# Thirty tiny probe loads in the stream of a decode block: one set of 15 amid the loads, one set behind the last

## The chip, the cores and the metric

The kernel runs on one NeuronCore of a Trainium2 chip. The metric is the device time of one execution in microseconds; the number given for a kernel is the median of its runs. A profile of one execution lies beside the times: it lists the instructions of the engines TensorE (PE), VectorE (DVE), ScalarE (ACT), GpSimd (POOL) and SyncE (SP), and the packets of the core's 16 DMA engines.

## The reference

One decode step (one token, batch 2, width 640) of a conditioned transformer block. Six modulation vectors come from a condition c; attention reads the last 1,024 of 4,096 cached positions, with 32 heads of 192; a gated FFN of width 1,536 follows. All inputs are bf16.

```python
def reference(A_x, A_k_cache, A_v_cache, A_wq, A_wo, B_x, B_w_gate, B_w_up, B_w_down, c, w_mod):
    # A: attention
    W = min(4096, max(256, Sk // 4))                     # 1024
    q = (h @ wq) per head
    k, v = k_cache[:, :, Sk - W:, :], v_cache[:, :, Sk - W:, :]
    p = softmax(einsum('bhqd,bhkd->bhqk', q, k) * Dh ** (-0.5))
    A = einsum('bhqk,bhkd->bhqd', p, v) reshaped @ wo
    # the block
    x = A_x
    mod = (silu(c) @ w_mod).reshape(2, 6, 1, -1)         # sa, ca, ga, sb, cb, gb
    h = layernorm(x) * (1 + ca) + sa
    x = x + ga * A(h)
    h = layernorm(x) * (1 + cb) + sb
    x = x + gb * ((gelu(h @ w_gate) * (h @ w_up)) @ w_down)
    return x
```

## The kernel before, in words

The kernel reads 76.9 MB from HBM once and does little with each byte: a K element is multiplied and summed, a V element and a weight are used in one matrix product. Nearly everything that is read goes into one big SBUF tile, `arena`, of seven slots, whose places are reused as soon as their contents are consumed.

There are 17 large loads, all issued by SP through `k_dma` (line 290), each over all 128 partitions. Their order is that of the dictionary `place`: w_mod; wq; the three pieces of K for batch 0, called k(0,0), k(0,1), k(0,2); then v(0,0), k(1,0), v(0,1), k(1,1), v(1,0), v(1,1); then wo, w_gate, w_up, and w_down in three pieces of 8, 3 and 1 row blocks (`WD_SPLIT`). A row of a load (one partition's share) is 1,280 to 61,440 B long. The function `pump` (line 333) writes the queue: it appends the next load to SP's list as long as the arena places that it overlaps have been named as consumed, and the recording class `_Sched` adds the wait on the engine that last used those places. SP runs its list strictly in order, so a load that waits holds up those behind it. Two tiny loads, c (`crow`, two rows) and x (`xr`, eight rows), and the store of the result (`st_out`, line 685) are issued by ACT.

Beside the stream the engines work as the data arrive. PE multiplies the modulation (line 454) and the query projection (line 486). For K, DVE multiplies a chunk by the broadcast query in place (line 512), PE sums it over the head's elements with an identity matrix (line 524), and DVE reduces the rest (line 531). Then comes the softmax of one batch (lines 536 to 555). For V, DVE spreads the probabilities over a mask (line 561) and PE multiplies (line 575). After v(1,1) come wo (line 634), the second layernorm, the gate and up products (line 655), the down product (line 675), two DVE steps (lines 681 and 683) and the store.

Every large load has a semaphore of its own, raised to 16 on completion. The four compute engines count on one semaphore each. At the end (lines 688 to 702) the waits are resolved, the first load is moved ahead of the entry barrier, and the lists are emitted engine by engine; SP gets a last wait for the store.

Of the kernel before, what the change touches and what calls it, by code (L numbers as in the profile page):

```python
# [8 lines left out]
BF16 = mybir.dt.bfloat16  # L9
# [110 lines left out]
def bass_adaLN_cond__sliding_block_cached__geglu_ffn__decode_kernel(  # L120
# [51 lines left out]
    WD_SPLIT = [(0, 8), (8, 3), (11, 1)]  # L172
# [15 lines left out]
    with es:  # L188
        S = _Sched(nc, es)
        sb = lambda name, shape, dt: es.enter_context(nc.sbuf_tensor(name, shape, dt))  # L190
# [10 lines left out]
        for kind, b, t, z in tiles:  # L201
            j0, n = (K_SPLIT if kind == "k" else V_SPLIT)[b][t]
# [86 lines left out]
        def k_dma(dst, src):  # L289
            return lambda e: e.dma_start(dst, src)  # L290

        items = list(place)
        assert items[0] == ("wm", 0)
        queue = {"next": 0, "done": set(), "ops": {}}

        def overlap(x, y):
            (a, m), (b, n) = place[x], place[y]
            return a < b + n and b < a + m

        def keys(it, lo=0, width=None):  # L300
            o, n = place[it]
            width = n - lo if width is None else width
            assert lo + width <= n
            return [("ar", z) for z in range((o + lo) // UNIT, -(-(o + lo + width) // UNIT))]

        def view(it, lo=0, width=None):
            o, n = place[it]
            width = n - lo if width is None else width
            return arena[:, o + lo:o + lo + width]

        def source(it):
            kind = it[0]
            if kind == "wm":
                return w_mod.rearrange("(p k) n -> p (k n)", k=KT)
            if kind == "wq":
                k0, n = WQ_SPLIT[it[1]]
                return A_wq.rearrange("(p k) n -> p (k n)", k=KT)[:, k0 * NQ:(k0 + n) * NQ]
            if kind == "wo":
                t0, n = WO_SPLIT[it[1]]
                return A_wo.rearrange("(p t) n -> p (t n)", t=NT)[:, t0 * D:(t0 + n) * D]  # L320
            if kind == "wg":
                return B_w_gate.rearrange("(p k) n -> p (k n)", k=KT)
            if kind == "wu":
                k0, nk = WU_SPLIT[it[1]]
                return B_w_up.rearrange("(p k) n -> p (k n)", k=KT)[:, k0 * F:(k0 + nk) * F]
            if kind == "wd":
                r0, nr = WD_SPLIT[it[1]]
                return B_w_down.rearrange("(p r) n -> p (r n)", r=FC)[:, r0 * D:(r0 + nr) * D]
            b, (j0, n) = it[1], span[it]
            src = A_k_cache if kind == "k" else A_v_cache  # L330
            return src[b][:, K0:Sk, :].rearrange("h (x j) d -> h x j d", x=XQ)[:, :, j0:j0 + n, :].rearrange("h x j d -> h x (j d)")

        def pump(*consumed):
            queue["done"].update(consumed)
            while queue["next"] < len(items):
                n = queue["next"]
                it = items[n]
                if not all(x in queue["done"] for x in items[:n] if overlap(x, it)):
                    break
                queue["ops"][it] = S.dma("sp", k_dma(view(it), source(it)), sem_of[it], writes=keys(it), name="ld_%s" % "_".join(str(z) for z in it))  # L340
                queue["next"] += 1

        pump()
        wm_dma = queue["ops"][("wm", 0)]
        S.op("pool", lambda e: e.memset(xr[:, :], 0.0), writes=["xr"], name="xr0")
# [102 lines left out]
        for half in range(2):  # L448
# [15 lines left out]
            if half == 0:  # L464
                ln_mod("ln1", 0, 0, hT)
        pump(("wm", 0))

        def out_rows(src, key, dst_t, name):
# [9 lines left out]
        for w, (k0, nk) in enumerate(WQ_SPLIT):  # L478
            def f(e, w=w, k0=k0, nk=nk):
                last = None  # L480
                wv = view(("wq", w)).rearrange("p (k i n) -> p k i n", k=nk, i=NR)
                for kk in range(nk):
                    k = k0 + kk
                    for n in range(NQB):
                        for i in range(NR):
                            last = e.matmul(ps[32 * i:32 * i + B, n, :], lhsT=hT[:, k, 0:RM:RB], rhs=wv[:, kk, i, n * QW:(n + 1) * QW],  # L486
                                            start=(k == 0), stop=(k == KT - 1), tile_position=(0, 32 * i))
                return last
            S.op("pe", f, reads=["ln1_out"] + keys(("wq", w)), writes=[bank(n) for n in range(NQB)], name="q1_%d" % w)
            pump(("wq", w))  # L490
# [205 lines left out]
        del body[n0:]  # L696
        body[entry:entry] = moved
        S.emit("sp", nc.sync, tail=lambda e: e.wait_ge(sem_out, 16))
        S.emit("pool", nc.gpsimd)
        S.emit("act", nc.scalar)  # L700
        S.emit("dve", nc.vector)
        S.emit("pe", nc.tensor)
        held, size = {}, None
# [41 lines left out]
```

## Time and profile before

| What | Value |
|---|---|
| Median of 3 runs | 185.7 us (185.64 to 185.83) |
| Span of the profiled execution, first to last instruction | 184.6 us |
| Difference of the median and this span | 1.1 us |
| Read from HBM | 76.88 MB, 417 GB/s over the span |
| PE busy | 106.4 us (58%) |
| DVE busy | 107.3 us (58%) |
| ACT, POOL busy | 14.4 us (8%), 6.1 us (3%) |
| Mean granted TensorE clock | 0.884 |
| DMA packets in the span | 2,495 |

The profiled execution's own time is its span of 184.6 us and what lies around it, before the first and after the last instruction; the page gives the span. A queue in the profile (q1 is SP's, q10 ACT's, q8 and q14 bring instructions) has a ring on each of the 16 DMA engines. A load shows there as its rows, one packet each, followed on every engine that takes part by a packet of 4 B, the completion write to the load's semaphore. An engine's packets of one queue run in the order of issue; packets of two queues take turns.

### The profile page before, as it was taken

How to read it: one execution, taken by the hardware profiler on the slowest of the kernel's cores; microseconds unless marked ns; L12 is line 12 of the kernel's file. 1: busy time of each engine (PE TensorE's matmuls, PEld its weight loads, DVE VectorE, ACT ScalarE, POOL GpSimd, SP SyncE). 2: the span in 40 equal slices, each digit the busy share in tenths (PEclk: the TensorE clock that was granted, in tenths of full speed). 3: DMA queues.
4: the chain of work that ended last, by engine and by line, in shares of the span. 5: the costliest groups of instructions: out<-in, count | busy, mean ns of one | idle time of the engine just before them, and what ended most of it. 6: DMA issues, size and time to landing. Idle time of an engine off the chain costs nothing.

```text
span 184.6 us, 1862 instructions
## 1 busy us (share of the span) xinstructions
PE 106.4 (58%) x960; PEld 28.9 (16%) x693; DVE 107.3 (58%) x105; ACT 14.4 (8%) x27; POOL 6.1 (3%) x23
## 2 busy tenths in 40 slices
PE   0019000948663096662499665946662499898833
PEld 0012000120000000001260001500001356405213
DVE  6022200049993488965993999489975838300631
ACT  2041100050000000001000000000001000220410
POOL 8400000000000000000000000000000000000000
PEclk9999955699999859999589999999998559999995
DMA  8999998999898989899898989898999999979991
GB/s 292 492 496 426 426 426 357 442 426 488 368 501 352 501 362 501 384 460 469 384 490 366 490 362 490 373 490 373 479 405 447 506 443 426 426 316 403 434 376 40
DMA packets 2495, 76.99 MB, mean 417 GB/s; under 512 B 310, under 2 KB 440, under 8 KB 568
## 3 DMA queue, kind: packets, MB, share of 16 engines
q1 hardware_dynamic: 2448, 76.87, 97.1%
q8 instruction: 6, 0.10, 0.2%
q10 hardware_dynamic: 40, 0.01, 0.0%
q14 instruction: 1, 0.01, 0.0%
HBM read 76.88 MB, written 0.00 MB: 417 GB/s over the span
## 4 chain that ended last, share of the span: by engine, by line
DMA 58%; DVE 24%; PE 16%; ACT 1%; issue 1%; SPq 0%
DMA arena<-in_A_k_cache_dram 36%; DMA arena<-in_B_w_down_dram 14%; DVE arena L512 14%; PE ps L575 8%; DMA arena<-in_w_mod_dram 8%; DVE S_sb L531 6%; PE ps L524 3%; DVE Em L561 2%; PE ps L454 2%; PE ps L675 1%; DVE negm L541 1%; ACT E_sb L549 1%; PE ps L552 1%; PE ps L545 0%; DVE M L537 0%
## 5 line engine op out<-in xcount | busy, mean ns | idle before, releaser
L524 PE MATMUL ps<-arena,ident_b 128*128 128x512 bf16 x192 | 48.9, 395 | 29.2 <-DVE arena L512 29.2
L512 DVE TENSOR_TENSOR arena<-arena,qbc 128x3072 bf16<-128x3072 bf16 x32 | 54.8, 1750 | 10.2 <-DMA arena<-in_A_k_cache_dram 8.5
L575 PE MATMUL ps<-arena,Em 128*64 128x384 bf16 x256 | 26.1, 374 | 5.6 <-DVE Em L561 5.6
L531 DVE TENSOR_REDUCE S_sb<-ps 128x32 f32<-128x1024 f32 x16 | 19.5, 1218 | 7.1 <-PE ps L524 7.1
L575 PEld LDWEIGHTS ps<-arena,Em 128*64 128x64 bf16 x256 | 16.2, 126 | 30.7 <-DVE Em L561 22.0
L561 DVE TENSOR_TENSOR Em<-E_sb,maskE 128x2048 bf16<-128x2048 bf16 x8 | 18.0, 2282 | 3.9 <-PE ps L575 3.9
L486 PE MATMUL ps<-arena,hT 128*2 128x512 bf16 x60 | 5.1, 517 | 14.0 <-DMA arena<-in_A_wq_dram 14.0
L496 DVE CAST qrow<-ps 128x512 bf16<-128x512 f32 x1 | 0.7, 691 | 17.4 <-PE ps L486 17.4
L539 PEld LDWEIGHTS ps<-ident_f,M 128*1 128x1 f32 x2 | 0.2, 79 | 61.1 <-DVE M L537 61.1
L408 PE MATMUL ps<-Em,ident_b 128*128 128x512 bf16 x41 | 9.3, 379 | 0.0
L641 DVE TENSOR_TENSOR lnt<-ps,modR 128x160 f32<-128x160 f32 x1 | 0.3, 323 | 12.7 <-PE ps L634 12.7
L549 ACT ACTIVATE E_sb<-S_sb,nbias 128x256 bf16<-128x256 f32 x2 | 1.0, 507 | 66.7 <-DVE nbias L547 66.7
L454 PE MATMUL ps<-arena,scT 128*17 128x480 bf16 x40 | 4.2, 602 | 2.1 <-DMA arena<-in_w_mod_dram 2.1
L582 ACT ACTIVATE On<-ps,rden 128x384 bf16<-128x384 f32 x2 | 1.2, 580 | 49.2 <-PE ps L575 49.2
L634 PEld LDWEIGHTS ps<-arena,oT 128*17 128x17 bf16 x192 | 3.3, 91 | 7.4 <-DMA arena<-in_A_wo_dram 7.4
L396 PE MATMUL ps<-ident_b,crow 2*128 2x2 bf16 x5 | 0.4, 177 | 6.5 <-DMA crow<-in_c_dram 6.5
L634 PE MATMUL ps<-arena,oT 128*17 128x160 bf16 x192 | 3.5, 233 | 0.6 <-DMA arena<-in_A_wo_dram 0.6
L417 PE MATMUL ps<-st,selstat 128*128 128x2 f32 x4 | 0.9, 298 | 4.9 <-ACT sqj L413 4.9
L401 DVE CAST X<-xr 128x160 f32<-128x160 bf16 x1 | 0.2, 243 | 5.8 <-DMA xr<-in_A_x_dram 5.8
L486 PEld LDWEIGHTS ps<-arena,hT 128*2 128x2 bf16 x20 | 0.6, 110 | 18.4 <-issue 18.4
L462 DVE TENSOR_SCALAR opc<-modR 128x160 f32<-128x160 f32 x2 | 0.5, 244 | 4.7 <-ACT modR L459 4.7
L655 PE MATMUL ps<-arena,h2T 128*9 128x384 bf16 x40 | 2.0, 326 | 1.9 <-DMA arena<-in_B_w_up_dram 1.3
(86 smaller groups left out, 51.1 us busy)
## 6 DMA issues: line engine op xcount, KB each, us to landing
arena<-in_A_v_cache_dram SPq DMA_DIRECT2D x4, 6144.0 KB, 26.3
arena<-in_A_k_cache_dram SPq DMA_DIRECT2D x3, 6144.0 KB, 37.5
arena<-in_A_wq_dram SPq DMA_DIRECT2D x1, 7680.0 KB, 31.5
arena<-in_A_wo_dram SPq DMA_DIRECT2D x1, 7680.0 KB, 29.2
arena<-in_A_k_cache_dram SPq DMA_DIRECT2D x2, 3072.0 KB, 42.2
arena<-in_w_mod_dram SPq DMA_DIRECT2D x1, 4800.0 KB, 14.2
arena<-in_B_w_gate_dram SPq DMA_DIRECT2D x1, 1920.0 KB, 21.2
arena<-in_B_w_up_dram SPq DMA_DIRECT2D x1, 1920.0 KB, 22.8
```

The lines of the kernel that those rows point to most:

```text
L408: last = e.matmul(ps[:, BK_T, :], lhsT=ident_b[:, :], rhs=Em[:, 0, 0:512 // H, :].rearrange("p j h -> p (j h)"), start=True, stop=True)
L454: last = e.matmul(ps[32 * i:32 * i + RM, half, 0:MH].rearrange("p (m n) -> p m n", n=DR), lhsT=scT[:, k, :], rhs=wv[:, 3 * half:3 * half + ...
L486: last = e.matmul(ps[32 * i:32 * i + B, n, :], lhsT=hT[:, k, 0:RM:RB], rhs=wv[:, kk, i, n * QW:(n + 1) * QW], start=(k == 0), stop=(k == K ...
L512: S.op("dve", lambda e: e.tensor_tensor(out=kt, in0=kt, in1=qbc[:, b, :].unsqueeze(1).broadcast_to([P, JC, Dh]), op=ALU.mult), reads=[("qb ...
L524: last = e.matmul(o_ap, lhsT=ident_b[:, :], rhs=kt[:, :, t * GC:(t + 1) * GC], start=(t == 0), stop=(t == NCH - 1))
L531: S.op("dve", lambda e: e.tensor_reduce(out=S_sb[:, b, 2 * JC * pair:2 * JC * (pair + 1)], in_=ps[:, 2 * z:2 * z + 2, :].rearrange("p k (j ...
L541: S.op("dve", lambda e: e.tensor_reduce(out=negm[:, b, :].rearrange("p (h x) -> p h x", x=XQ), in_=ps[0:1, BK_T, 0:P].rearrange("p (h x) - ...
L549: S.op("act", lambda e: e.activation(out=E_sb[:, b, :], in_=S_sb[:, b, :], func=ACTF.Exp, scale=SCALE, bias=nbias[:, b:b + 1], accum_out=d ...
L561: S.op("dve", lambda e, z=z, j=j: e.tensor_tensor(out=Em[:, z, :, :], in0=E_sb[:, b, j:j + JE].unsqueeze(2).broadcast_to([P, JE, H]), in1= ...
L575: last = e.matmul(ps[64 * i:64 * i + 2 * H, BK_O, 0:ON], lhsT=Em[:, z, 2 * jp:2 * jp + 2, :].rearrange("p j h -> p (j h)"), rhs=view(it, l ...
L634: last = e.matmul(ps[32 * i:32 * i + RM, 2, 0:DR], lhsT=oT[:, t, :], rhs=wv[:, t, i, :], start=(t == 0), stop=(t == NT - 1), tile_position ...
L655: last = e.matmul(ps[32 * i:32 * i + GM, bk, 0:FT], lhsT=h2T[:, k, 0:RM:2], rhs=wv[:, k, i * FT:(i + 1) * FT], start=(k == 0), stop=(k == ...
```

## The change

A small tile `prb` of 17 partitions is added, and a function `probe`, which issues one load of k rows of 32 B each (16 elements of the first k rows of w_mod) into a place of its own, with a semaphore of its own. After the issue of v(0,0) and again after the issue of the last piece of w_down, `pump` calls it 15 times on SP, for 17 rows, then 2, 3, and so on up to 15 rows. Nothing reads `prb`. So that the program doesn't end before these loads, POOL waits at its end for the first 15 semaphores, and ACT, behind the store's issue, for the other 15.

```diff
+        prb = sb("prb", [17, 30, 16], BF16)
+        probes = []
+
+        def probe(eng, k):
+            n = len(probes)
+            sem = S.sem("d_prb%d" % n)
+            probes.append(sem)
+            S.dma(eng, k_dma(prb[0:k, n, :], w_mod[0:k, 0:16]), sem, writes=[("prb", n)], name="prb%d" % n)
+
         items = list(place)
...
                 queue["ops"][it] = S.dma("sp", k_dma(view(it), source(it)), sem_of[it], writes=keys(it), name="ld_%s" % "_".join(str(z) for z in it))
                 queue["next"] += 1
+                if it in (("v", 0, 0), ("wd", len(WD_SPLIT) - 1)):
+                    for k in (17,) + tuple(range(2, 16)):
+                        probe("sp", k)
...
         S.emit("sp", nc.sync, tail=lambda e: e.wait_ge(sem_out, 16))
-        S.emit("pool", nc.gpsimd)
-        S.emit("act", nc.scalar)
+        S.emit("pool", nc.gpsimd, tail=lambda e: [e.wait_ge(x, 16) for x in probes[:15]])
+        S.emit("act", nc.scalar, tail=lambda e: [e.wait_ge(x, 16) for x in probes[15:]])
```

SP's list grows from 17 loads to 47. The instructions of the other engines keep their order; POOL and ACT each get 8 waiting instructions at their ends, of which all but one wait for two semaphores.

## The prediction

> **What bounds the kernel now.** I read the page's DMA rows first, then its chain, then SyncE's (SP's) waits and DMA issues, and last the individual packet records behind the page (start, length, size and queue of each DMA packet), because the change consists of packets.
>
> From the page (DMA busy share in tenths by slice; queue, packets, MB, share of 16 engines; the chain):
>
> ```profile
> DMA  8999998999898989899898989898999999979991
> ...
> q1 hardware_dynamic: 2448, 76.87, 97.1%
> q8 instruction: 6, 0.10, 0.2%
> q10 hardware_dynamic: 40, 0.01, 0.0%
> ...
> DMA 58%; DVE 24%; PE 16%; ACT 1%; issue 1%; SPq 0%
> ```
>
> The kernel is one uninterrupted stream on q1, SP's queue: 97.1% of all 16 engines' span, and the missing 3% is the first microsecond and the last five. The chain's 24% DVE and 16% PE are work beside the stream: it follows buffer releases back, and those releases come early. The table by stretch confirms it (stretch, length, then busy time by engine, clock, DMA share, GB/s):
>
> ```profile
> 54.00:84.00 30.00, 17.17 (x60) 0.00 (x0) 21.80 (x16) 0.00 (x0) 0.00 (x0) 0.89 1.01 436
> 84.00:150.00 66.00, 42.09 (x260) 12.26 (x168) 52.38 (x39) 1.78 (x5) 0.00 (x0) 0.89 1.01 436
> ```
>
> DMA share 1.01 at 436 GB/s: nothing else limits these 96 us. So the end is set by the DMA engine that finishes its share of the last load last. SP's part of the timeline and the groups of line L290 give the room at the two insertion points (start and length in us; below, min/median/max ns of one issue):
>
> ```profile
> 37.58 0.54 SPq L290 DMA_DIRECT2D arena<-in_A_v_cache_dram  x1
> 53.92 0.53 SPq L290 DMA_DIRECT2D arena<-in_A_k_cache_dram  x1
> ...
> 154.75 1.39 SPq L290 DMA_DIRECT2D arena<-in_B_w_down_dram  x3
> ```
> ```profile
> L290 ACTq DMA_DIRECT2D crow<-in_c_dram x1: 535/535/535, 0.8 to 0.8; - x1
> L290 ACTq DMA_DIRECT2D xr<-in_A_x_dram x1: 637/637/637, 1.4 to 1.4; - x1
> ...
> L290 ACTq DMA_DIRECT2D out_dram<-finb x1: 662/662/662, 182.8 to 182.8; - x1
> ```
>
> The tail, from the timeline:
>
> ```profile
> 180.42 1.79 PE L675 MATMUL ps<-arena,aT 128*25 128x80 bf16 x96 [2.20 <-DMA arena<-in_B_w_down_dram]
> 182.25 0.24 DVE L681 TENSOR_TENSOR fin<-ps,go 128x80 f32<-128x80 f32 x1 [2.75 <-PE ps L675]
> 182.53 0.24 DVE L683 TENSOR_TENSOR finb<-fin,xo 128x80 bf16<-128x80 f32 x1
> 182.80 0.66 ACTq L290 DMA_DIRECT2D out_dram<-finb  x1
> ```
>
> In the packet records the third w_down load reports from its 16 engines between 179.3 and 181.42 us; matmul, two DVE steps and the store follow the last report and end the span at 184.56.
>
> **Who is last, and by how much.** Packets on one engine follow each other without a gap, so one engine can be followed from packet to packet. All engines do equal work (8 rows of each load); three things set them apart. First, their start: first packets begin at 0.99 to 1.15 us on 13 engines, but at 1.24, 1.55 and 1.87 us on three. Second, the packets of q10 (c and x), at 16 to 52 ns each. Third, instruction packets: each 16,384 B packet of q8 holds one engine up for 1.4 to 1.56 us, and one of 8,192 B for about 1.0 us. Six fell on six different engines (16,384 B at 43.1, 98.4, 150.1, 165.7 and 173.2 us, 8,192 B at 78.6); the sixth of q8, at 181.3, finds its engine done. At the end:
>
> - the engine that began at 1.55 and was hit at 150.1: 181.42, the last
> - the other four hit by 16 KB: 181.17, 181.16, 181.07, 180.99
> - the one hit by 8 KB: 180.65; the one that began at 1.87: 180.17
> - the other nine: 179.4 to 179.7
>
> c (2 rows) used two engines and x four, the two of c among them. Call these 0 to 3, with 0 and 1 the pair of c. Engines 0 and 1 end at about 179.5, 1.87 us ahead of the last. One of 2 and 3 ends at 179.72; the other is one of two that I cannot tell apart, at 180.65 or 181.17. So the last engine is one of 4 to 15.
>
> **The change, part by part.** It removes nothing and moves nothing. It adds 30 loads of 32 B per row to SP, and 15 waits each to the ends of POOL and ACT (built as 8 instructions of two waits on each). PE's, DVE's, ACT's and POOL's rows are otherwise the same in the same order.
>
> *Issues of the first set on SP.* They stand between the issues of v(0,0) and k(1,0), which begin at 37.58 and 53.92. Fifteen at 0.54 to 0.66 us, plus the 0.04 us between issues, are 8.7 to 10.5 us; they end at 38.12 + 10.5 = 48.6 at the latest, while SP is waiting for PE anyway. Cost 0. If an issue took over 1.05 us, k(1,0) would be issued late, and even that is covered: the ring is busy with v(0,0) until its first engine reports at 74.78. The cover is gone only beyond 2.4 us an issue.
>
> *Issues of the second set.* They follow w_down's third issue, end at 156.14 + 10.5 = 166.6, and nothing but SP's last wait is behind them (it waits 28.4 us for the store). Cost 0.
>
> *The first set on the engines.* This is the only part on the path: it lies in the ring between v(0,0) and k(1,0), and the stream has no gap to hide it. A load of k rows puts one row and one completion write on each of k engines, if it spreads as c and x did: engine 1 gets 14 pairs, engine e from 2 upward 15 - e, engine 15 none. The 17-row load I put wholly on engine 0, the worst place: 17 + 14 = 31 rows and 15 completion writes. Price of a pair: a completion write moves the next packet by 6 ns (wherever one load ends and the next begins). No 32 B row is in the trace; the nearest are the store's 160 B (12 ns long, so 9 ns of ring after the usual 3 ns overlap), the 320 B of x (16 ns) and the 1,280 B of w_down (52 ns). So a pair costs 15 ns by the nearest and 58 ns by the farthest; I take 15, because the length falls with the size all along these rows. A gain has no mechanism here.
>
> - Engine 0: 31 x 9 + 15 x 6 = 0.37 us, at most 31 x 52 + 90 = 1.70 us. Both are under its 1.87 us lead: hidden.
> - Engine 2 or 3, if it is the one at 181.17: 13 x 15 = 0.20 us, to 181.37, still behind the leader's 181.42; by 58 ns 0.75 us, to 181.92, or 0.50 past it.
> - The last engine, somewhere in 4 to 15: 0 to 11 pairs, 0 to 0.17 us, 0.08 in the middle; by 58 ns 0 to 0.64 us, 0.32 in the middle.
>
> Sum on the path: 0.1 us, bounds 0 and 0.64. What is late next is still the third w_down load.
>
> *The second set on the engines.* It is behind w_down in every ring, so delays no data. Engine 0 would need to work past 184.1, when the store's packets run, to meet anything: 4.6 us after its 179.5, against 0.37 to 1.70. The end probes of the last engine land 0.2 us after 181.42.
>
> *The waits.* POOL has nothing else after 7.3 us. ACT's stand behind the store's issue (ends 183.47); nothing is queued behind them. Eight at the 17 ns that SP's own last wait took are 0.14 us, to 183.6, inside the 184.55 at which SP sees the store.
>
> [...] First the row: three w_down loads follow each other on every engine with 6 ns between the last packet of one and the first of the next; no load pays a start-up of its own. [...]
>
> **The numbers.** The profiled span is 184.56 us; the median run, 185.7, is 1.1 above it, for what lies around the span, and the change does not touch that. 185.7 + 0.1 = **185.8 us**. A measurement here can tell about 0.2%, 0.37 us, from no change.
>
> **The rivals.**
>
> *A. Tiny reads run at the pace of their latency (slower).* In before no more than eight small rows follow each other, and all could have been read ahead. The first packets of the kernel took 2.24 us instead of 1.42, so a cold read needs about 0.82 us. The 3,840 B rows kept a pace of 146 ns, so at least 0.82/0.146 = 6 reads are in flight. With just 6, a 32 B row costs 137 ns: engine 0 would lose 31 x 137 = 4.2 us, 2.4 past the leader (188.1 us), the last engine 0 to 1.5. It decides from about 57 ns a row on engine 0 (1.87 us less 90 ns, by 31), or, if the last engine is number 6 (9 pairs), from 41 ns a pair (0.37/9). For: 31 rows in a row is something that before never shows. Against: the pace at 1,280 B was the wire's, with no sign of a limit. Chance 0.22.
>
> *B. Instruction packets fall on other engines.* The lead of 1.9 us is theirs. If they land elsewhere in the new program, the end moves: 0.25 earlier if the late starter is spared (185.45), 0.3 later if the engine that began at 1.87 is hit (186.0), 1.4 later if one engine is hit twice (187.1). For: six packets decide everything. Against: three runs within 0.19 us say that the places repeat, and PE's program, by far the longest, is unchanged. Chance 0.17.
>
> *C. The loads do not spread and name nothing:* all on one engine. In one set 17 + 2 + 3 + ... + 15 = 136 rows, at 9 ns with 15 completion writes 1.3 us: hidden on engine 0, and the time is 185.7. Chance 0.06.
>
> **How the numbers follow.** Forecast 0.55, nearly all within 0.2% (its upper bound of 0.64 us gives 0.03 to slower). A gives 0.22 to slower. B splits into 0.04 faster, 0.03 the same and 0.10 slower; C is the same. Together: faster 0.04, the same 0.61, slower 0.35. The range runs from 185.4 (B's early end) to 187.2 (B's double hit and the smaller part of A); A's larger part is left out.
>
> **What would show it.** The packet records should show the first set between 74.8 and 77 us, 15 ns a pair, engine 0 gone from the stream for 0.4 us; completions from 1, 2, 3 ... 15 engines in turn; k(1,0) issued at about 53.9 as before; w_down's last report at 181.4 to 181.6; ACT's waits over before the store lands. Rows of 32 B at 60 ns or more, or an engine among 0 to 3 reporting last, would be A; instruction packets on other engines, B. The prediction is wrong if the last report moves by over 0.4 us, or if something ends after the store.

## The result, and the profile after

The changed kernel takes 187.02 us (median of 3 runs, 186.97 to 187.03) against 185.70: a ratio of 1.007, 95% interval 1.005 to 1.0089. That is 1.3 us slower, clear of the 0.37 us that can be told from no change, inside the range and on the side that I gave 0.35.

The page of the changed kernel, DMA share by slice, queues and chain:

```profile
DMA  8999998999899998999999999999999999989981
...
q1 hardware_dynamic: 2960, 76.88, 97.0%
q8 instruction: 6, 0.10, 0.2%
q10 hardware_dynamic: 40, 0.01, 0.0%
...
DMA 58%; DVE 22%; PE 18%; ACT 1%; issue 1%; SPq 0%
```

The 512 new packets on q1 are the probes, 272 rows and 240 completion writes. The engines count as busy as before. The table by stretch tells more (stretch, length, busy time by engine, clock, DMA share, GB/s):

```profile
54.00:84.00 30.00, 17.16 (x64) 0.00 (x0) 23.04 (x17) 0.00 (x0) 0.00 (x0) 0.89 0.99 417
84.00:150.00 66.00, 40.16 (x244) 10.70 (x152) 51.45 (x38) 1.78 (x5) 0.00 (x0) 0.87 1.00 433
```

The stretch with the first set moves 417 GB/s instead of 436 at a DMA share of 0.99: the rows that are stretched there, up to 3.65 us long instead of 1.82, count as busy over their whole length. SP's timeline and its groups:

```profile
38.50 0.54 SPq L290 DMA_DIRECT2D arena<-in_A_v_cache_dram  x1
39.08 6.34 SPq L290 DMA_DIRECT2D prb<-in_w_mod_dram  x15
54.82 0.54 SPq L290 DMA_DIRECT2D arena<-in_A_k_cache_dram  x1
...
158.48 17.81 SPq L290 DMA_DIRECT2D prb<-in_w_mod_dram  x15
```
```profile
L290 SPq DMA_DIRECT2D prb<-in_w_mod_dram x30: 247/511/2235, 39.1 to 175.3; - x30
```

The first set is issued in 6.34 us, long before k(1,0) has to be issued. The tail, by the timeline:

```profile
181.58 1.82 PE L687 MATMUL ps<-arena,aT 128*25 128x80 bf16 x96 [2.18 <-DMA arena<-in_B_w_down_dram]
183.46 0.24 DVE L693 TENSOR_TENSOR fin<-ps,go 128x80 f32<-128x80 f32 x1 [2.77 <-PE ps L687]
183.74 0.24 DVE L695 TENSOR_TENSOR finb<-fin,xo 128x80 bf16<-128x80 f32 x1
184.01 0.66 ACTq L290 DMA_DIRECT2D out_dram<-finb  x1
```

Every line of the tail stands 1.2 us later, with lengths within 0.03 us of those before: the whole loss is in the stream, ahead of w_down's end. The span is 185.8 against 184.6.

**Where it is lost.** In the packet records the probes take what a look at their size suggests: 6 ns a packet, 11.8 ns a pair, with no gap, between 74.7 and 76.7 us. But the first row of k(1,0) behind them, 49,152 B and 1.82 us long in the kernel before, takes up to 3.65 us. By engine (numbered by the probes, each engine matched by the length of its series) the first row of k(1,0) is stretched by (some engines left out):

| Engine | Loads on it | Stretch, us |
|---|---|---|
| 0 (31 rows) | 15 | 1.84 |
| 1 | 14 | 1.70 |
| 3 | 12 | 1.43 |
| 5 | 10 | 1.26 |
| 7 | 8 | 0.96 |
| 8 | 7 | 0.45 |
| 9 | 6 | 0.25 |
| 10 | 5 | 0.11 |
| 11 to 15 | 4 to 0 | under 0.03 |

**Who is last now.** Engine 5. It had been held up by the instruction packet at 43.2 us, and ran some 1.5 us behind the others when the probes came. In the kernel before, the engine hit at that time ended at 181.07; 0.12 us of pairs and 1.26 us of stretch make that 182.45, and the third w_down load reports at 182.53 from an engine on which ten pairs of the second set follow, which is engine 5. The probes name it directly: a load of k rows completes on one engine more than the load of k - 1 rows, and in the first set the completion that is new with the load of 6 rows comes at 77.26, when all earlier ones of that load are in by 76.42. Engines 0 to 4 lost more, but their leads took it up: 0 to 2 report at 181.41 to 181.44, 3 at 182.17 and 4 at 180.72.

### The profile page after: what moved, and what is told of

Its sections match the earlier page's. It is cut to its first block, busy times and chain, and to the rows that moved or that the text cites. A ratio compares the mean times of both kernels' runs of the same rounds, so it can differ in the third digit from the quotient of the medians.

```text
span 185.8 us, 1908 instructions
## 1 busy us (share of the span) xinstructions
PE 106.5 (57%) x960; PEld 28.7 (15%) x693; DVE 107.5 (58%) x105; ACT 14.4 (8%) x27; POOL 6.1 (3%) x23
## 4 chain that ended last, share of the span: by engine, by line
DMA 58%; DVE 22%; PE 18%; ACT 1%; issue 1%; SPq 0%
DMA arena<-in_A_k_cache_dram 38%; DMA arena<-in_B_w_down_dram 13%; DVE arena L524 12%; PE ps L587 8%; DMA arena<-in_w_mod_dram 8%; DVE S_sb L543 6%; PE ps L536 5%; DVE Em L573 2%; PE ps L466 2%; PE ps L687 1%; DVE negm L553 1%; ACT E_sb L561 1%; PE ps L564 1%; PE ps L557 1%; DVE M L549 0%
## 5 line engine op out<-in xcount | busy, mean ns | idle before, releaser
L587 PE MATMUL ps<-arena,Em 128*64 128x384 bf16 x256 | 25.3, 365 | 5.7 <-DVE Em L573 5.7
L498 PE MATMUL ps<-arena,hT 128*2 128x512 bf16 x60 | 6.1, 598 | 14.4 <-DMA arena<-in_A_wq_dram 14.4
L687 PE MATMUL ps<-arena,aT 128*25 128x80 bf16 (+1 forms) x96 | 1.8, 265 | 2.2 <-DMA arena<-in_B_w_down_dram 2.2
## 6 DMA issues: line engine op xcount, KB each, us to landing
arena<-in_A_k_cache_dram SPq DMA_DIRECT2D x2, 3072.0 KB, 42.2
```

Source lines behind the costliest of these rows:

```text
L587: last = e.matmul(ps[64 * i:64 * i + 2 * H, BK_O, 0:ON], lhsT=Em[:, z, 2 * jp:2 * jp + 2, :].rearrange("p j h -> p (j h)"), rhs=view(it, l ...
L687: last = e.matmul(ps[32 * i:32 * i + m, BK_OT, CY:CY + OC], lhsT=aT[:, 32 * fc + a:32 * fc + a + m], rhs=wv[:, i, h, :], start=(fc == WD_S ...
```

## The experiments

All kernels compute the whole reference. The diffs are cut to the lines that matter and are against the changed kernel; all but "end_only" and the last leave the second set out, as "mid_only" does. The waits of a set that is left out go with it; in "end_only" ACT waits for all 15 loads. Medians beside them are of the kernel before on the same chip.

**One set alone.**

```diff
-                if it in (("v", 0, 0), ("wd", len(WD_SPLIT) - 1)):
+                if it == ("v", 0, 0):                  # mid_only
+                if it == ("wd", len(WD_SPLIT) - 1):    # end_only
```

> Only the first set of 15 loads, behind v(0,0); the second set and its waits are left out. Three theories. Theory 1, starved row, by loads: the small packets themselves go out at 6 ns each, but an engine that has run through many small loads in a row has nothing read ahead, and the first large row behind them (k(1,0)) waits for its data; the loss grows with the number of loads on the engine: none up to four, about 1.0 us at eight, 1.7 at fourteen. Theory 2, the same, but by the number of rows. Theory 3: nothing waits; the larger program makes instruction packets fall on other engines. Theories 1 and 2 expect the whole change: 187.0 us, eleven stretched rows in k(1,0) of up to 3.65 us instead of 1.82, and the third w_down load ending near 182.5 us. Theory 3 expects another time, since the program is 15 loads shorter, anywhere from 185.4 to 187.1.

Measured: 186.91 us, ratio 1.0058 (1.0041 to 1.0075). Eleven rows of k(1,0) are stretched by 0.07 to 1.79 us.

> Only the second set of 15 loads, behind w_down; the first set is left out. Theories 1 and 2: no large row stands behind these loads, so nothing can be starved: 185.7 us, within 0.2 us of the kernel before, and no row of k(1,0) over 1.83 us except beside an instruction packet. Theory 3: the program has as many loads as in the run with the first set alone, so the same time as that run.

Measured: 185.86 us against 185.86, ratio 0.9997 (0.9988 to 1.0006); no row is stretched. Within the noise the first set is the whole loss, and theory 3 falls: two programs of equal length differ by 1.05 us, and the rows are stretched in one of them alone.

**Loads or rows.** For both, `prb` gets 128 partitions.

```diff
-                    for k in (17,) + tuple(range(2, 16)):
+                    for k in (P, P):         # two_by_128: 16 rows, 2 loads on every engine
+                    for k in (16,) * 15:     # fifteen_by_16: 15 rows, 15 loads on every engine
```

> The first set is replaced by two loads of 128 rows of 32 B: 16 rows and two completion writes on each of the 16 engines; no second set. Theory 1 (loads count): two loads are under the four that cost nothing; 18 packets at 6 ns are 0.11 us on every engine: 185.8 us and no stretched row. Theory 2 (rows count): 16 rows are more than the 14 that cost 1.7 us, on every engine, the last one too: 185.7 + 1.7 + 0.1 = 187.5 us. Theory 3: 185.8 or a shift by instruction packets.

Measured: 186.11 us, ratio 1.0015 (1.0005 to 1.0024); the first rows of k(1,0) are longer by 0.01 to 0.07 us, 0.05 on average.

> The first set is replaced by 15 loads of 16 rows of 32 B: 15 rows and 15 completion writes on each of the 16 engines; no second set. Theories 1 and 2 expect every engine to lose what the fullest ones lost in the changed kernel, 1.8 us, and 0.18 us for 30 packets: the whole stream ends 2.0 us later, 187.7 us, with 16 stretched rows of about 3.6 us in k(1,0). Theory 3: 0.18 us at most, 185.9.

Measured: 188.01 us, ratio 1.0115 (1.010 to 1.013). All 16 first rows are stretched, by 1.57 to 2.37 us, 1.89 on average; with 0.18 us of packets that is 2.07 an engine, and the median is 2.15 us later. About as many rows, 16 against 15, lose 0.05 or 1.89 us: the loads count, the rows don't. The stretch from 74 to 93 us, of the kernel before, of the run with two loads and of the run with fifteen:

```profile
74.00:93.00 19.00, 10.01 (x48) 2.53 (x25) 15.28 (x14) 0.60 (x2) 0.00 (x0) 0.85 0.99 427
```
```profile
74.00:93.00 19.00, 10.01 (x48) 2.53 (x25) 15.27 (x14) 0.60 (x2) 0.00 (x0) 0.84 0.98 420
```
```profile
74.00:93.00 19.00, 10.01 (x50) 2.55 (x27) 14.55 (x13) 0.60 (x2) 0.00 (x0) 0.82 0.98 373
```

The DMA share hardly differs (0.99, 0.98, 0.98); the rate is 427, 420 and 373 GB/s.

**The lead of an engine.**

```diff
-                    for k in (17,) + tuple(range(2, 16)):
+                    for k in (2,) * 15:      # fifteen_by_2
```

> The first set is replaced by 15 loads of 2 rows, on engines 0 and 1 alone; no second set. Theory 1 has two halves, and this tests the second: the loss counts only where the engine has no lead. On engines 0 and 1 the row behind should be stretched as with 15 loads of 16 rows, by 1.6 to 2.4 us, so each loses about 2.0 us; but these two led the last engine by 1.87 us in the kernel before, so the end moves by 0 to 0.3 us: 185.7 to 186.0. If any stretched row moves the end (the consumers of k(1,0), say, are what matters), it is 187.5 or more.

Measured: 186.0 us against 185.83, ratio 1.0017 (1.0003 to 1.0031), though two rows are stretched by 1.97 and 2.09 us. A loss of more than 2 us on engines 0 and 1 costs 0.2 at the end: only what exceeds an engine's lead counts. In the profiled execution (186.34 us) the engine with 2.09 is itself the last and reports at 181.90, the other of the two at 181.42, and the last engine without small loads at 181.26.

**The dose.**

```diff
-                    for k in (17,) + tuple(range(2, 16)):
+                    for k in (16,) * 8:      # eight_by_16
```

> The first set is replaced by 8 loads of 16 rows of 32 B, so 8 rows and 8 completion writes on every engine; no second set. Theory 1 by its own dose in the changed kernel (0.96 us on the engine with 8 pairs, 0.45 with 7): every engine loses about 1.0 us and 0.1 us for the packets, 186.8 us. If the loss came only with long series (a queue that overflows at ten or more), 185.8.

Measured: 186.57 us, ratio 1.0037 (1.0025 to 1.005). All 16 rows are stretched, by 0.48 to 0.96 us, 0.71 on average, so 0.81 an engine with the packets; I had expected about 1.0 and 0.1. The loss does not begin only at ten loads.

**The same loads, not in a row.**

```diff
+        GAPS = {("v", 0, 0): (17, 2), ("k", 1, 0): (3, 4), ("v", 0, 1): (5, 6), ("k", 1, 1): (7, 8),
+                ("v", 1, 0): (9, 10), ("v", 1, 1): (11, 12), ("wo", 0): (13, 14), ("wg", 0): (15,)}
...
-                if it == ("v", 0, 0):
-                    for k in (17,) + tuple(range(2, 16)):
+                if it in GAPS:
+                    for k in GAPS[it]:
                         probe("sp", k)               # spread
```
```diff
                 if it == ("v", 0, 0):                  # act_queue: one set, as in mid_only
                     for k in (17,) + tuple(range(2, 16)):
-                        probe("sp", k)
+                        probe("act", k)
```

> The same 15 loads as the first set, but two at a time, behind each of eight large loads from v(0,0) to w_gate; no second set. Theory 1: never more than two small loads in a row on an engine, so nothing is starved: no stretched row except beside an instruction packet, and 185.7 to 185.9 us (0.01 to 0.18 us of packets on an engine). If each small load had a fixed price of its own, whatever stands before it, the end would be that of the first set alone, 186.9 us.

Measured: 185.89 us against 185.83, ratio 0.9998 (0.9989 to 1.0007). One row of k(1,0) is longer by 0.1 us, none other except beside instruction packets.

> The same 15 loads as the first set, issued by ACT ahead of its copies of the query, so on the other queue; no second set. Large rows and small ones then take turns on each engine. Theory 1: a small row between two large ones starves nothing, so no stretched row and 185.7 to 185.9 us. If the engine's read ahead is shared and emptied by any 15 small loads in flight, stretched rows and about 186.9 us.

Measured: 185.90 us, ratio 1.0001 (0.9992 to 1.001). The 256 packets of the set stand on ACT's queue:

```profile
q1 hardware_dynamic: 2448, 76.87, 97.0%
...
q10 hardware_dynamic: 296, 0.01, 0.1%
```

Four large rows are longer by 0.07 to 0.19 us, none by more, except beside instruction packets and at the start of the stream. The price belongs to the series, not to the single load.

**What in a load costs.** Four theories of it were left: the small reads themselves, reads of one address (every load so far read the same rows), HBM's answer, and the rows' size, 32 B so far.

```diff
-            ... k_dma(prb[0:k, n, :], w_mod[0:k, 0:16]) ...                  # fifteen_by_16
+            ... k_dma(prb[0:k, n, :], w_mod[16 * n:16 * n + k, 256 * n:256 * n + 16]) ...   # fifteen_distinct
+            ... k_dma(prb[0:k, n, :], ident_b[0:k, 0:16]) ...                # fifteen_sbuf
+            ... k_dma(prb[0:k, n, :], w_mod[0:k, 0:256]) ...                 # fifteen_512, prb a view of Em
```

> As the run with 15 loads of 16 rows, but each load reads 16 other rows of w_mod, so no 32 B are read twice; in the runs so far every load read the same first rows, and an engine read one address 15 times. Theory 1 (the load is what costs): the same, all 16 engines with a stretched row in k(1,0) of 3.4 to 4.2 us instead of 1.82. Theory 4 (reads of one address queue up in memory; two loads of 128 rows were cheap because their rows differ): no stretched row, 186.0 us.

Measured, one run: 187.87 us; 16 rows stretched by 1.47 to 2.39 us, 1.91 on average. Not the addresses.

> As the run with 15 loads of 16 rows, but the source is a tile in SBUF (the identity matrix) instead of w_mod in HBM. If what delays the row behind is HBM's answer to each small read, the stretch shrinks clearly below the 1.6 to 2.4 us of the HBM source; if it is the handling of a load on the engine's queue, whatever it reads, it stays within that.

Measured, one run: 188.34 us; 1.56 to 2.39 us, 1.92 on average. Not HBM's answer to a read; and that small reads alone do not cost it, the run with two loads of 128 rows showed (16 reads an engine, 0.05 us).

> As the run with 15 loads of 16 rows, but rows of 512 B instead of 32 B, written to a tile that is not yet in use. Theory 1: each load takes its time on the queue beside the packets, so longer packets fill the same time: the packets take 0.4 us instead of 0.18, and the stretch falls by about as much, to some 1.2 to 2.1 us; their sum stays at about 2.0 us. If rows under 512 B are what is expensive, no stretch remains and the sum is 0.4 us.

Measured, one run: 188.5 us; 1.33 to 2.32 us, 1.78 on average, only 0.11 less than with 32 B, though the packets now take 0.50 us an engine instead of 0.18. Neither expectation holds: the rows' size is not what costs, and longer packets fill little of the time. Nothing here supports the "read ahead" of theory 1. What is left of it is that the time goes by the number of loads in a row.

The landings of the probes' semaphores show where it goes. The packets of 15 loads leave an engine within 0.18 us, but its completions do not land so. On the last engine of fifteen_by_16 they land at 77.57, 77.74, 77.95 and so on to 80.02 us, 0.165 to 0.208 apart, 0.175 on average; the median engine shows 0.18. In the runs with other addresses, SBUF as the source, 512 B rows or eight loads it is about 0.20 on the last engine and 0.18 to 0.19 on the median one. POOL's waits show it too. They are eight instructions, and they end at 78.83 to 80.04, right behind the last landings of the 8th to the 15th load (78.81 to 80.02), one load further each:

```profile
L711 POOLq EVENT_SEMAPHORE  x8: 17/43/43, 78.8 to 80.0; - x8
```

Seven loads further in 1.2 us (78.83 to 80.04) are 0.17 us a load. So the completions of the loads follow each other on an engine far more slowly (0.175 us apart) than the packets that the records show (0.18 us for all 30).

The same landings tell what the large row waits for. With the engines sorted by time, the first row of k(1,0) ends 0.62 to 0.65 us after the last landing of its engine's series, on all 16 engines in the runs with fifteen loads of 16 rows (other addresses, SBUF and 512 B rows included) and in that with eight, and on the eleven stretched engines of the changed kernel. Behind one large load, in the kernel before, it ends 1.30 to 1.37 us after that load's landing. The row's end is thus tied to the end of the series, though part of the row, 1.82 us long when nothing delays it, moves before that. What in a load's completion takes the 0.18 us, no run separates. What an engine loses in the changed kernel (stretch and packets together) follows roughly 0.19 us a load less 0.75 us, an estimate fitted to these numbers: 1.91 against 1.87 measured at 14 loads, 0.58 against 0.54 at 7, 0.20 against 0.17 at 5; it is 0.3 us low at 8 loads and 0.2 at the ten of engine 5 (1.15 against 1.38). In the runs with equal engines it gives 2.10 (measured 2.07) at 15 loads and 0.77 (0.81) at 8. By this estimate 0.75 us, about four completions, are hidden, and the landings show nearly that room: from 1.35 us behind a landing, where an undelayed row ends, to 0.63.

**Both sets, the first one spread.** spread_full has the gaps of spread and the second set behind w_down.

> The whole of the change with its first set spread: two loads behind each of eight large loads, and the second set of 15 behind w_down, with both sets of waits at the ends of POOL and ACT. Theory 1: as the kernel before, 185.7 to 185.9 us, with no stretched row except beside an instruction packet; all 30 loads are done before the store. If the 30 loads and their waits have a price together that neither set shows alone, more than 186.2.

Measured: 185.93 us against 185.94, ratio 1.0003 (0.9993 to 1.0012). All 30 loads and their waits are free when they are not in a row ahead of data.

## Why the prediction was right or wrong

**The range** held the time, 187.02 in 185.4 to 187.2, but by luck: its upper part was there for rivals A and B, neither of which happened as described, and the sum itself gave 185.8, at most 186.3 by its own bound of 0.64. By the prediction's own sign it failed, since the last report moved by 1.11 us, from 181.42 to 182.53, and not by 0.4 at most.

**What bounds the kernel** held: the end moved with the engine of the stream that is last, and nothing else.

**SP's issues** held for the first set: 0.25 to 0.5 us each, one of 1.24, all before k(1,0). For the second set I had 0.66 us at most an issue and the end at 166.6; they took 0.29 to 2.24 us and ended at 176.3. Nothing was behind them, so the error cost nothing. The last of the set landed at 185.05, 2.5 us after w_down's last report, where I had 0.2; the store was seen only at 185.75.

**The price of a pair** was right as far as it went: 11.8 ns against 15.

**The step that failed** is the sum of the first set's time on the engines, 0.1 us with bounds 0 and 0.64. I took the ring time of the packets for the whole price. The ground was the row of the three w_down loads, 6 ns from one to the next, from which I concluded that no load pays a start-up of its own. That row shows three loads in a row, and up to four are indeed free (the row behind is longer by under 0.03 us); at ten the row behind pays 1.26 us. I carried a row from three to fifteen without asking what it showed of fifteen. And I read the packets' starts alone: the landing times of the semaphores, which are also in the trace, were not looked at. The term measured 1.38 us (0.12 of pairs, 1.26 of stretch) on engine 5, of which 0.35 only brought that engine level with the one that had been last.

**The last engine** changed with it. I costed the engine that had started late and was hit at 150.1; engine 5 was 0.35 us ahead of that one, with ten loads. Among engines 4 to 15 I gave numbers for the last one alone, and none for the other engines hit by 16 KB, 0.25 to 0.43 us ahead of it.

**Rival A** was right in its direction, and in that a series of many small loads does what a short one doesn't show. Its form was wrong: no row took 137 ns (all 272 of 32 B took 9), the wait is not for HBM's reads (with SBUF as the source the stretch is 1.92 us, with HBM 1.89), 31 rows in 15 loads lost little more than 14 rows in 14 loads (1.84 and 1.70), and engine 0 was not the one that decided.

**Rival B** did not happen as described: each instruction packet before the last report hit another engine once, at 43.2 engine 5, at 80.3 engine 3, at 97.8 engine 6. That its double hit, 187.1 us, is close to what was measured is chance. Two programs of equal length, one set each, settle it.

**Rival C** fell: the loads do what they say. That the load of 17 rows goes to one engine was my supposition, which no row of the kernel before shows; now its semaphore shows one landing of data (75.46 us), that of the load of 2 rows two, that of 15 rows fifteen, each new one on the next engine. One more event comes right after the issue (at 40.04 us for the load of 2 rows, issued by 39.87). As the waits for 16 ended (POOL's last one at 79.1, behind the last landing at 79.10), the rest of the 16 should have come with that event; the trace gives its time and not its amount.

**A price of a load's own**, which I denied on the row of three w_down loads, was denied too completely: one or two loads between large ones cost nothing that can be told (185.89 against 185.83 us in spread), fifteen in a row 0.14 us each (2.07 us an engine in fifteen_by_16).

**ACT's waits** I had at 0.14 us; they took from 184.71 to 185.27, 0.077 us a step, and still ended before the store was seen at 185.75.

## What to carry to other kernels

Small loads in one queue were free here one or two at a time between large ones (185.89 against 185.83 us), and cost about 0.19 us each beyond the fourth when they stood in a row ahead of data: spread them, put them on the other queue (185.90), or behind the last data (185.86 against 185.86). Packets that follow each other without a gap don't show that nothing waits: look at when the semaphores land (0.175 us apart here, with 12 ns of packets a load), at the length of the packet behind the series (up to 3.65 us instead of 1.82), and at GB/s where the DMA share is already full (373 instead of 427, at shares of 0.98 and 0.99). In a kernel bound by its stream like this one, the engine that is last sets the time, so a delay is priced on that engine: 2 us lost on two engines with a lead of 1.87 us cost 0.2 (fifteen_by_2).

## What the runs showed of the hardware that I had not expected

- Completions of consecutive loads land 0.17 to 0.21 us apart on an engine, whether the rows have 32 or 512 B and come from HBM or from SBUF, while the packet records of loads with 32 B rows are 6 ns apart.
- SP's issue of a small load takes 0.25 to 0.49 us in the first set, one of 1.24 apart, and up to 2.24 us behind w_down: in the second set the second to fourth took 1.67, 2.23 and 2.24 us, the last two near the length of one row of wo (2.27 us). What sets these times, no run shows.
- Instruction packets fall at nearly the same times in most kernels (42.2 to 44.5, 76.6 to 81.0 and 97.8 to 100.2 us for the first three; in the run with 512 B rows the second came at 91.4) and hold up one engine each by about 1.5 us (16 KB) or 0.9 to 1.0 (8 KB). Together with the start of the stream they make the 2 us by which the last engine is behind the first (179.3 to 181.42 us in the kernel before).
